# Scores and values on parts of the PE array, pairs of blocks grouped by mode, one array and one transfer for each block

## The chip, the cores and the metric

The kernel runs on one core of a Trainium2 chip. The time is device microseconds of that core, taken without the profiler's help from whole executions. Each kernel also has one profiled execution. Engines: PE is the TensorE matmul, PEld its weight load, DVE VectorE, ACT ScalarE, POOL GpSimd.

## The reference, cut to what matters

Chunked attention, then a mixture of experts with a locality gate. The change touches the attention alone, and what stands between it and the first expert.

```python
# q, k, v: (4 batches, 8 heads, 768, 64); chunk 32, left context 16, right context 8, 8 memory rows
for c in range(seq // 32):
    k_full = concat(mem_k, k[l_start:r_end]);  v_full = concat(mem_v, v[l_start:r_end])
    a = softmax(q[chunk] @ k_full.T / 8);      out[chunk] = a @ v_full
x = out as (4, 768, 512)
for b, s:                                      # routing, one token after the other
    e = argmax(x @ w_gate) if s == 0 or sigmoid(x @ w_local) < 0.5 else the expert of s - 1
    out[b, s] = softmax(x @ w_gate)[e] * (relu(x[b, s] @ w1[e]) @ w2[e])
```

## The kernel before

The kernel works on 32 blocks of three chunks (96 queries). A block's keys are laid out so that 128 rows serve its three chunks. For each block PE computes scores transposed (keys in the partitions), ACT takes the exponential, PE multiplies by the values, which carry a column of ones for the sum, and DVE divides. Blocks go in pairs for the scores, and the routing of a half batch (four blocks) is spread over later blocks. Cut to what the change and the argument touch:

```python
def scores(qt, kt, qb):
    s_ps = sps.tile([P, 2, 512], F32, name="s_ps")
    st = s_ps[:, :, 0:HP * QB].rearrange("p u (a n) -> p u a n", a=HP)
    for a in range(HP):                       # HP = 4 pairs of heads
        for u in range(2):                    # a head's 64 dims: rows 0-63 or 64-127
            h = slice(DH * u, DH * u + DH)
            nc.tensor.matmul(st[:, u, a], lhsT=kt[h, a], rhs=qt[h, a], start=True, stop=True)
    ...                                       # exponentials on ScalarE into pt

def values(pt, vt, n, x):
    for u in range(2):
        o_ps = ops.tile([QB, HP, VW], F32, name="o_ps", tag=f"o_ps{u}")      # one buffer for each half
        for a in range(HP):
            nc.tensor.matmul(o_ps[:, a], lhsT=pt[:, u, a], rhs=vt[:, 2 * a + u], start=True, stop=True)
        rinv = rinvs[:, n, u]
        nc.vector.reciprocal(rinv, o_ps[:, :, DH:VW])
        nc.vector.tensor_tensor(...)          # x = o_ps * rinv

def route_places(r, half):
    nc.vector.tensor_tensor(rank[:, h], rank[:, h], onehot[:, h], op=ALU.mult)
    ...

for n in range(NB):                           # NB = 32 blocks, PAIR = 2
    if n % PAIR == 0:
        for f in first.pop(n, ()): f()        # logits of four finished blocks
        for m in range(n + PAIR, min(n + 2 * PAIR, NB)):
            begun[m] = begin(m)               # scores of the next pair
    ...
    values(begun.pop(n), vts.pop(n), n, xs[b][0:QB, j])
    ...
    if n > 0:
        turn(n - 1)                           # transposes of the block before, and ScalarE's copy
    for f in after.pop(n, ()): f()            # steps of the routing, early plan, first gathers
```

PE's instructions are kept in program order. After the attention come the expert tiles. The rows of the first five are gathered by GpSimd's indirect transfers while the attention still runs.

## Time and profile before

| | before |
|---|---|
| timed runs | 533.83 us, median of 3 (526.76 to 535.96) |
| profiled run | 500.6 us, span 498.5 us, mean granted clock 0.994 |
| PE busy | 485.0 us of the span (97%), 3474 matmul records and as many weight loads |
| attention's end (first expert product, h_ps) | 112.7 us |

### The profile page before, as it was taken

The numbers are of one execution on the slowest core, as the hardware profiler recorded it, in microseconds if no ns is written. First come the engines' busy times: TensorE is split into PE (matmuls) and PEld (weight loads), VectorE is DVE, ScalarE is ACT, GpSimd is POOL, SyncE is SP. The second block draws the span as 40 slices with busy tenths as digits, with TensorE's granted clock in tenths as the row PEclk, the third lists the DMA queues.
The fourth block names the chain that finished last, engine by engine and source line by source line (L and its number), as shares of the span: only waits on it lengthen the run. The fifth ranks groups of instructions, "written<-read, shape, count | busy, mean of one in ns | idle before, by whom it ended". The sixth has DMA issues, their size and how long they took to land. (4 is left out here: it accounts for less than half of the span.)

```text
span 498.5 us, 9231 instructions
## 1 busy us (share of the span) xinstructions
PE 485.0 (97%) x3474; PEld 371.5 (75%) x3474; DVE 109.4 (22%) x437; ACT 111.1 (22%) x234; POOL 99.0 (20%) x151
## 2 busy tenths in 40 slices
PE   8999999999999999999999999999999999999993
PEld 5998888888766777766677776667777666958761
DVE  2456677775435000001000000000000000000000
ACT  4555555542111111111111111110111110201110
POOL 3003222433341122110111111001102110031301
PEclk9999999999999999999999999999999999999997
DMA  8987899999999999998999899995169999921101
GB/s 284 384 268 230 280 280 288 313 352 392 409 328 393 410 408 400 350 313 318 336 333 332 318 322 322 331 339 214 39 214 413 373 400 410 393 70 52 45 29 31
DMA packets 49377, 146.01 MB, mean 293 GB/s; under 512 B 7258, under 2 KB 11358, under 8 KB 49312
## 3 DMA queue, kind: packets, MB, share of 16 engines
q1 hardware_dynamic: 42240, 123.38, 68.6%
q0 software_dynamic: 6784, 21.30, 11.7%
q8 instruction: 34, 0.56, 0.5%
q10 hardware_dynamic: 288, 0.52, 0.3%
q14 instruction: 31, 0.25, 0.1%
HBM read 132.57 MB, written 13.00 MB: 292 GB/s over the span
## 5 line engine op out<-in xcount | busy, mean ns | idle before, releaser
L644 PE MATMUL y_ps<-w_sb,ht 128*128 128x512 f32 x224 | 98.5, 593 | 0.0
L644 PEld LDWEIGHTS h_ps<-held_xt,w_sb 128*128 128x128 f32 x704 | 80.5, 192 | 6.6 <-issue 4.9
L644 PE MATMUL h_ps<-held_xt,w_sb 128*128 128x128 f32 x704 | 81.3, 275 | 0.9 <-ACTq _compat.py:109 0.9
L644 PEld LDWEIGHTS y_ps<-w_sb,ht 128*128 128x128 f32 x224 | 41.5, 190 | 46.9 <-issue 46.6
L796 POOL DMA_INDIRECT out_dram<-y,to x24 | 24.2, 1010 | 240.3 <-ACT y L795 213.2
L780 PEld LDWEIGHTS h_ps<-gxt,w_sb 128*128 128x128 f32 x448 | 51.2, 192 | 2.9 <-issue 2.9
L780 PE MATMUL h_ps<-gxt,w_sb 128*128 128x128 f32 x448 | 51.7, 275 | 0.0
L783 ACT ACTIVATE ht<-h_ps 128x512 f32<-128x512 f32 x42 | 25.1, 597 | 118.9 <-PE h_ps L644 78.1
L791 PE MATMUL y_ps<-w_sb,ht 128*128 128x512 f32 x112 | 49.4, 592 | 0.0
L644 PE MATMUL o_ps<-vt,pt 128*96 128x65 f32 x512 | 49.2, 249 | 0.1
L644 PEld LDWEIGHTS o_ps<-vt,pt 128*96 128x96 f32 x512 | 46.2, 165 | 2.2 <-DVE x L358 0.6
L466 POOL DMA_INDIRECT x_dram<-x,row x32 | 29.6, 926 | 73.9 <-DVE x L464 59.0
L710 DVE COPY held_xt<-g_ps 128x512 f32<-128x512 f32 x12 | 8.3, 689 | 137.5 <-PE g_ps L644 123.0
L791 PEld LDWEIGHTS y_ps<-w_sb,ht 128*128 128x128 f32 x112 | 20.7, 190 | 23.0 <-issue 22.2
L644 PEld LDWEIGHTS s_ps<-qt,kt 64*128 64x128 f32 x512 | 30.2, 189 | 6.8 <-issue 4.6
L644 PE MATMUL s_ps<-qt,kt 64*128 64x96 f32 x512 | 33.0, 279 | 0.4 <-ACT pt L348 0.4
L644 PEld LDWEIGHTS h_ps<-x,w_sb 128*128 128x128 f32 x192 | 31.2, 190 | 1.2 <-issue 1.2
L644 PE MATMUL h_ps<-x,w_sb 128*128 128x192 f32 x192 | 31.9, 327 | 0.0
L348 ACT ACTIVATE pt<-s_ps,mask_mid 128x256 f32<-128x256 f32 x72 | 28.1, 482 | 7.1 <-PE s_ps L644 7.0
L710 DVE COPY gxt<-g_ps 128x512 f32<-128x512 f32 x10 | 6.9, 690 | 95.5 <-PE g_ps L707 52.8
L795 ACT ACTIVATE y<-y_ps,x 128x512 f32<-128x512 f32 x12 | 8.3, 688 | 83.1 <-PE y_ps L644 76.4
L358 DVE TENSOR_TENSOR x<-o_ps,rinvs 96x256 f32<-96x256 f32 x64 | 26.3, 418 | 1.2
(207 smaller groups left out, 375.4 us busy)
## 6 DMA issues: line engine op xcount, KB each, us to landing
w_sb<-in_w_dram SPq DMA_DIRECT2D x192, 512.0 KB, 8.9
vt<-in_v_dram SPq DMA_DIRECT2D x32, 260.0 KB, 4.7
kt<-in_k_dram SPq DMA_DIRECT2D x30, 256.0 KB, 4.9
qt<-in_q_dram SPq DMA_DIRECT2D x32, 192.0 KB, 4.3
kt<-in_k_dram ACTq DMA_DIRECT2D x2, 256.0 KB, 3.3
x_dram<-x,row POOLq DMA_INDIRECT x32, 7.2
out_dram<-y,to POOLq DMA_INDIRECT x24, 7.1
x<-x_dram,rows_late POOLq DMA_INDIRECT x11, 7.2
```

Source lines behind the costliest of these rows:

```text
L348: nc.scalar.activation(pt[:, :, :, c], st[:, :, :, c], ACT.Exp, bias=m[:, g:g + 1], scale=SCALE)
L358: nc.vector.tensor_tensor(x[:, 0:D].rearrange("p (a u d) -> p u a d", u=2, d=DH)[:, u], o_ps[:, :, 0:DH], rinv.to_broadcast([QB, HP, DH]), ...
L466: ins = nc.gpsimd.indirect_dma_start(out=x_dram[:, :], out_offset=bass.IndirectOffsetOnAxis(ap=row[:, n:n + 1], axis=0), in_=x[0:QB, j + n ...
L644: return lambda *a, **k: tc.keep_in_program_order(f(*a, **k))
L710: nc.vector.tensor_copy(xt[:, :, 0:P], g_ps)
L780: nc.tensor.matmul(h_ps[:, m], lhsT=w1_sb[:, kk, P * (g + m):P * (g + m) + P], rhs=xt[:, kk, 0:rows], start=(kk == 0), stop=(kk == DK - 1))
L783: nc.scalar.activation(ht[:, g:g + many], h_ps, ACT.Relu)
L791: nc.tensor.matmul(y_ps, lhsT=ht[:, m, 0:P], rhs=w2_sb[:, m], start=(m == 0), stop=(m == FK - 1))
L795: nc.scalar.activation(y, y_ps, ACT.Copy, scale=xs[:, D:D + 1])
L796: return nc.gpsimd.indirect_dma_start(out=out, out_offset=bass.IndirectOffsetOnAxis(ap=to, axis=0), in_=y, in_offset=None, bounds_check=NT ...
```

## The change

The intent: use the small products better. The scores have only 64 rows to contract, so the array is split into four 64x64 tiles. The values have 96 columns of weights, so they go on three tiles of 32 columns. As a change of tile mode drains PE (from scores to values before, 202 ns pass from last start to first start, against 85 ns within the values), the order is regrouped: both blocks' values, then both transposes, then the routing's transposes. A block's q, k and v become one array and one transfer. Two smaller parts: the ranks are transposed with all 128 rows, and one multiplication of the routing moves from VectorE to GpSimd.

```diff
 def scores(qt, kt, qb):
         for a in range(HP):
-            for u in range(2):
-                h = slice(DH * u, DH * u + DH)
-                nc.tensor.matmul(st[:, u, a], lhsT=kt[h, a], rhs=qt[h, a], start=True, stop=True)
+            for c in (slice(0, DH), slice(DH, P)):
+                for u in range(2):
+                    h = slice(DH * u, DH * u + DH)
+                    nc.tensor.matmul(st[c, u, a], lhsT=kt[h, a, c], rhs=qt[h, a], start=True, stop=True,
+                                     tile_position=(DH * u, c.start))
 def values(pt, vt, n, x):
             for a in range(HP):
-                nc.tensor.matmul(o_ps[:, a], lhsT=pt[:, u, a], rhs=vt[:, 2 * a + u], start=True, stop=True)
+                for g in range(NG):
+                    c = slice(CHUNK * g, CHUNK * g + CHUNK)
+                    nc.tensor.matmul(o_ps[c, a], lhsT=pt[:, u, a, c], rhs=vt[:, 2 * a + u], start=True, stop=True,
+                                     tile_position=(0, CHUNK * g))
 def route_places(r, half):
-        nc.vector.tensor_tensor(rank[:, h], rank[:, h], onehot[:, h], op=ALU.mult)
+        nc.gpsimd.tensor_tensor(rank[:, h], rank[:, h], onehot[:, h], op=ALU.mult)
 def route_rows(r, b, half, x):
-        r_ps = xps.tile([QB, HALF, E], F32, name="r_ps", tag="xps")
+        r_ps = xps.tile([QB, HALF, P], F32, name="r_ps", tag="xps")
-            nc.tensor.transpose(r_ps[:, n], rank[:, ...], identity=ident[:E, :E])
+            nc.tensor.transpose(r_ps[:, n], ranks[:, ...], identity=ident)
 ... (q, k, v as slices of one array qkv; one transfer for each block but the first two)
-    plan_at(after, NB - 3, first_turned)
+    plan_at(after, NB - 2, first_turned)
-    for n in range(NB):
-        ... (logits; scores of the next pair; then for each block: values, transposes, routing)
+    for n in range(0, NB, PAIR):
+        pair = range(n, n + PAIR)
+        for m in range(n + PAIR, min(n + 2 * PAIR, NB)):
+            begun[m] = begin(m)
+        for m in pair:
+            ...
+            values(begun.pop(m), blocks.pop(m)[2], m, xs[b][0:QB, j])
+            ...
+            for f in first.pop(m, ()): f()        # logits, between the two blocks' values
+        for m in range(max(n - 1, 0), n + PAIR - 1):
+            turn(m)
+        for m in pair:
+            for f in after.pop(m, ()): f()
```

More of the change, by code (lines that the diff above doesn't have):

```diff
@@ L46 @@
 LOADS = 6
+KEYS = HP * QB
+VALS = KEYS + HP * P
+BW = VALS + H * VW
 PLAN = 3 * E + 5
@@ L66 @@
     tc: tile.TileContext,
-    q: bass.AP,
-    k: bass.AP,
-    v: bass.AP,
+    qkv: bass.AP,
     w_gate: bass.AP,
@@ L88, with general @@
     nc.gpsimd.iota(back, pattern=[[0, 1], [1, E]], base=-E, channel_multiplier=0, allow_small_or_imprecise_dtypes=True)
-    everything(tc, q, k, v, w_gate, w_local, w1, w2, x_dram, out, ident, back, kept_i)
+    everything(tc, qkv, w_gate, w_local, w1, w2, x_dram, out, ident, back, kept_i)
     kept = nc.values_load(kept_i, min_val=0, max_val=NT * H, skip_runtime_bounds_check_because="a count of sums")
     with tc.If(kept < NT * H):
-        general(tc, q, k, v, w_gate, w_local, w1, w2, out, ident, back)
+        general(tc, qkv, w_gate, w_local, w1, w2, out, ident, back)
 @with_exitstack
-def general(ctx, tc, q, k, v, w_gate, w_local, w1, w2, out, ident, back):
+def general(ctx, tc, qkv, w_gate, w_local, w1, w2, out, ident, back):
     nc = tc.nc
@@ L131, in general @@
             qt, kt, vt = (one.tile([P, a, w], F32, name=t) for t, a, w in (("qt", HP, QB), ("kt", HP, P), ("vt", H, VW)))
-            for t, a in ((qt, q), (kt, k), (vt, v)):
-                nc.sync.dma_start(t, a[n])
+            for t, at in ((qt, 0), (kt, KEYS), (vt, VALS)):
+                _, a, w = t.shape
+                nc.sync.dma_start(t, qkv[n, :, at:at + a * w].rearrange("p (a w) -> p a w", a=a))
             x = one.tile([QB, HP, 2, DH], F32, name="x")
@@ L232, in everything @@
 @with_exitstack
-def everything(ctx, tc, q, k, v, w_gate, w_local, w1, w2, x_dram, out, ident, back, kept_i):
+def everything(ctx, tc, qkv, w_gate, w_local, w1, w2, x_dram, out, ident, back, kept_i):
     nc = tc.nc
@@ L259, in everything, with block, parts, load @@
     nc.gpsimd.dma_start(x_dram[0:1], zeros[0:1].bitcast(I32))
-    def load_qk(n, queue=nc.sync):
-        qt = ld.tile([P, HP, QB], F32, name="qt")
-        nc.sync.dma_start(qt, q[n])
-        kt = ld.tile([P, HP, P], F32, name="kt")
-        queue.dma_start(kt, k[n])
-        return qt, kt
-    def load_v(n):
-        vt = ld.tile([P, H, VW], F32, name="vt")
-        nc.sync.dma_start(vt, v[n])
-        return vt
-    qks = {n: load_qk(n, nc.scalar) for n in range(2)}
-    qks.update({n: load_qk(n) for n in range(2, LOADS - 2)})
-    vts = {n: load_v(n) for n in range(LOADS - 2)}
+    def block():
+        return ld.tile([P, BW], F32, name="block")
+    def parts(t):
+        q, k, v = t[:, 0:KEYS], t[:, KEYS:VALS], t[:, VALS:BW]
+        return (q.rearrange("p (a w) -> p a w", a=HP), k.rearrange("p (a w) -> p a w", a=HP),
+                v.rearrange("p (h w) -> p h w", h=H))
+    def load(n):
+        t = block()
+        nc.sync.dma_start(t, qkv[n])
+        return parts(t)
+    blocks = {}
+    for n in range(PAIR):
+        t = block()
+        nc.sync.dma_start(t[:, 0:KEYS], qkv[n, :, 0:KEYS])
+        nc.scalar.dma_start(t[:, KEYS:VALS], qkv[n, :, KEYS:VALS])
+        blocks[n] = t
+    for n in range(PAIR):
+        nc.sync.dma_start(blocks[n][:, VALS:BW], qkv[n, :, VALS:BW])
+        blocks[n] = parts(blocks[n])
+    blocks.update({n: load(n) for n in range(PAIR, LOADS)})
     wg = once.tile([P, DK, QUARTER], F32, name="wg")
@@ L332, in everything @@
                             base=0, channel_multiplier=-1)
+    ranks = once.tile([P, S], F32, name="ranks")
+    nc.gpsimd.memset(ranks, 0.0)
     def scores(qt, kt, qb):
@@ L432, in route_ranks @@
         of_half = slice(HQ * half, HQ * half + HQ)
-        if half == 0:
-            r["rank"] = sm.tile([E, S], F32, name="rank")
-        onehot, rank = r["onehot"], r["rank"]
+        onehot, rank = r["onehot"], ranks[0:E]
         nc.vector.tensor_tensor_scan(rank[:, of_half], onehot[:, of_half], onehot[:, of_half],
@@ L442, in route_places @@
     def route_places(r, half):
-        onehot, rank = r["onehot"], r["rank"]
+        onehot, rank = r["onehot"], ranks[0:E]
         h = slice(HQ * half, HQ * half + HQ)
-        nc.vector.tensor_tensor(rank[:, h], rank[:, h], onehot[:, h], op=ALU.mult)
+        nc.gpsimd.tensor_tensor(rank[:, h], rank[:, h], onehot[:, h], op=ALU.mult)
         tot = r["tot"] = sm.tile([QB, HALF, 1], F32, name="tot")
@@ L454, in route_rows @@
         j = HALF * half
-        rank, tot, ex = r["rank"], r["tot"], r["ex"][:, j:j + HALF]
-        r_ps = xps.tile([QB, HALF, E], F32, name="r_ps", tag="xps")
+        tot, ex = r["tot"], r["ex"][:, j:j + HALF]
+        r_ps = xps.tile([QB, HALF, P], F32, name="r_ps", tag="xps")
         for n in range(HALF):
-            nc.tensor.transpose(r_ps[:, n], rank[:, QB * (j + n):QB * (j + n) + QB], identity=ident[:E, :E])
+            nc.tensor.transpose(r_ps[:, n], ranks[:, QB * (j + n):QB * (j + n) + QB], identity=ident)
+        r_ps = r_ps[:, :, 0:E]
         row = sm.tile([QB, HALF], I32, name="row", bufs=2)
@@ L649, in begin @@
     def begin(n):
-        ahead = n + LOADS - 2
-        if ahead < NB:
-            qks[ahead] = load_qk(ahead)
-        return scores(*qks.pop(n), n % NQB)
+        return scores(*blocks[n][0:2], n % NQB)
     xs, xts, lts, routes = {}, {}, {}, {}
@@ L734, in everything @@
     begun = {n: begin(n) for n in range(PAIR)}
-    for n in range(NB):
-        b, j = divmod(n, NQB)
-        if n % PAIR == 0:
-            for f in first.pop(n, ()):
-                f()
-            for m in range(n + PAIR, min(n + 2 * PAIR, NB)):
-                begun[m] = begin(m)
-        if j == 0:
-            xs[b] = xp.tile([P, NQB, XW], F32, name="x")
-            nc.gpsimd.tensor_copy(xs[b][0:QB, :, D + 1:XW].bitcast(I32), token[:, n:n + NQB])
-            routes[b] = begin_route()
-        if j % HALF == 0:
-            xts[n // HALF] = sm.tile([P, DK, HALF, QB], F32, name="xt", bufs=2)
-        values(begun.pop(n), vts.pop(n), n, xs[b][0:QB, j])
-        if n + LOADS - 2 < NB:
-            vts[n + LOADS - 2] = load_v(n + LOADS - 2)
-        if n > 0:
-            turn(n - 1)
-        for f in after.pop(n, ()):
-            f()
+    for n in range(0, NB, PAIR):
[3 more added lines that the diff above has]
+        for m in pair:
+            b, j = divmod(m, NQB)
+            if j == 0:
+                xs[b] = xp.tile([P, NQB, XW], F32, name="x")
+                nc.gpsimd.tensor_copy(xs[b][0:QB, :, D + 1:XW].bitcast(I32), token[:, m:m + NQB])
+                routes[b] = begin_route()
+            if j % HALF == 0:
+                xts[m // HALF] = sm.tile([P, DK, HALF, QB], F32, name="xt", bufs=2)
+            values(begun.pop(m), blocks.pop(m)[2], m, xs[b][0:QB, j])
+            if m + LOADS < NB:
+                blocks[m + LOADS] = load(m + LOADS)
+            for f in first.pop(m, ()):
+                f()
+        for m in range(max(n - 1, 0), n + PAIR - 1):
+            turn(m)
+        for m in pair:
+            for f in after.pop(m, ()):
+                f()
     some_pieces(len(early["pieces"]))
@@ L962 @@
     arrays = {
-        "q": dims_first(i["q"]).reshape(B, P, HP, NQB, QB).transpose(0, 3, 1, 2, 4).reshape(NB, P, HP, QB),
-        "k": dims_first(with_mem["k"])[..., bands].transpose(0, 3, 1, 2, 4).reshape(NB, P, HP, P),
-        "v": rows(with_mem["v"])[:, bands].reshape(NB, P, H, VW),
+        "qkv": _np.concatenate([
+            dims_first(i["q"]).reshape(B, P, HP, NQB, QB).transpose(0, 3, 1, 2, 4).reshape(NB, P, HP * QB),
+            dims_first(with_mem["k"])[..., bands].transpose(0, 3, 1, 2, 4).reshape(NB, P, HP * P),
+            rows(with_mem["v"])[:, bands].reshape(NB, P, H * VW)], 2),
         "w_gate": i["moe_w_gate"],
```

## The prediction

> **What bounds the kernel now.** I first read the page's table of busy time in slices: TensorE (PE) is at nine tenths in nearly every slice, and the clock there is full. Then the table of windows: from 0 to about 112 us the attention runs (scores, exponentials, values, routing), and from there to the end the expert tiles, in which PE is busy 10.00 of every 10 us. The change touches only the attention; the expert tiles keep their instructions. So I looked at PE's own timeline over four blocks, the period of the routing:
>
> ```profile
> 53.19 2.03 PE L644 MATMUL s_ps<-qt,kt 64*128 64x96 f32 x32
> 55.15 1.57 PE L644 MATMUL o_ps<-vt,pt 128*96 128x65 f32 x16
> 56.56 0.50 PE L644 MATMUL xt_ps<-ident,x 96*128 96x96 f32 x4
> 56.99 0.35 PE L644 MATMUL r_ps<-ident,rank 8*96 8x8 f32 x4
> 57.63 0.64 PE L644 MATMUL l_ps<-ident,lt_sb 128*96 128x128 f32 x4 [0.29 <-ACT xt L366]
> 58.11 1.49 PE L644 MATMUL o_ps<-vt,pt 128*96 128x65 f32 x16
> 59.44 0.50 PE L644 MATMUL xt_ps<-ident,x 96*128 96x96 f32 x4
> 59.87 2.03 PE L644 MATMUL s_ps<-qt,kt 64*128 64x96 f32 x32
> ...
> 65.77 0.85 PE L644 MATMUL lt_ps<-xt,wg 128*32 128x384 f32 x8
> ```
>
> Columns: start, duration, then the group. The period from scores to scores of four blocks is 53.19 to 66.56, that is 13.37 us, and PE hardly waits in it. Values of one block (o_ps) and of the next are apart by a transpose (xt_ps) and sometimes more. What VectorE (DVE) does with them in the meantime is this:
>
> ```profile
> 56.08 0.18 DVE L357 RECIPROCAL rinvs<-o_ps 96x4 f32<-96x4 f32 x1 [1.19 <-PE o_ps L644]
> 56.29 0.42 DVE L358 TENSOR_TENSOR x<-o_ps,rinvs 96x256 f32<-96x256 f32 x1
> 56.76 0.18 DVE L357 RECIPROCAL rinvs<-o_ps 96x4 f32<-96x4 f32 x1
> 56.97 0.42 DVE L358 TENSOR_TENSOR x<-o_ps,rinvs 96x256 f32<-96x256 f32 x1
> ```
>
> Each half block (u) costs DVE 0.68 us from reciprocal to reciprocal. Each o_ps half has only one PSUM buffer, so the next block's half 0 may start only when L358 has read this block's. Today it starts 1.75 us after it at the closest, and the DVE chain takes about 1.6: it just fits. The third view is the list of groups by shape:
>
> ```profile
> L644 PE MATMUL o_ps<-vt,pt 128*96 128x65 f32 x512 | 49.2, 249 | 0.1
> L644 PE MATMUL s_ps<-qt,kt 64*128 64x96 f32 x512 | 33.0, 279 | 0.4 <-ACT pt L348 0.4
> L644 PE MATMUL yu_ps<-w_sb,x 128*64 128x256 f32 x96 | 11.0, 382 | 0.0
> L644 PE MATMUL lt_ps<-xt,wg 128*32 128x384 f32 x64 | 6.8, 498 | 0.3
> ```
>
> Each product is two instructions (256 score products, 512 records). yu_ps and lt_ps are column tiles already in use.
>
> **What the Trainium skill says.** "TensorE: Matmul & The Clock Gate", section "LDWEIGHTS (loading the stationary operand)", puts a weight load at its columns divided by 1.2 GHz: 80 ns for 96, 107 for 128. The trace agrees: in steady state o_ps instructions start 85 ns apart, and pairs of score instructions 112 ns apart, so both are bound by weight loads, not by streaming 65 or 96 columns. "TensorEngine Tiling (Array Packing)", section "Tiling Modes", says that tiles load and multiply in parallel and that a change of mode drains the engine. The trace agrees: the two column halves of yu_ps start 7 ns apart, one pair every 215.7 ns; lt_ps starts its four quarters 7 ns apart; and where the mode changes, scores to values, 202 ns pass from last start to first start instead of 85. The same page, "PSUM Bottleneck", warns that evacuation may become the limit once the matmuls are faster. This is what I expect here, though no line of before shows it yet.
>
> **The change part by part.** All is for four blocks, two pairs, against 13.37 us.
>
> Scores on 64x64 tiles: four tiles start together. Streaming 96 columns takes 80 ns (yu_ps gives 215.7 for 256, so 0.84 ns a column), loading 64 columns less. One group of four every 84 ns in place of a pair every 112: 16 groups a pair of blocks, 1.28 us to the last start in place of 1.757. Saved: 0.47 a pair, 0.95 in four blocks.
>
> Values on 128x32 tiles: a load of 32 columns is 27 ns, streaming 65 columns 55 to 57. Three tiles every 57 ns in place of one instruction every 85: a half takes 0.46 us in place of 0.68. On PE alone that would be 8 halves x 0.22 = 1.8 us in four blocks. But the changed order puts both blocks' values back to back, and DVE's order of instructions is reciprocal, product, reciprocal, product as before. Counting from the first values instruction T: half 0's last start at T+0.42; DVE takes it up 0.285 later (as the trace has it) at T+0.72, ends at T+1.35; the next block's half 0 starts at T+1.40 instead of T+0.92. Half 1 is done by DVE at T+2.03, the next block's half 1 runs T+2.08 to T+2.5. So the four halves take about 2.5 us, the same as the 2.57 they took before. The gain on values is nearly all lost to DVE.
>
> Grouping by mode: logits (lt_ps) now sit between the two blocks' values, in the same mode, where PE waits for DVE anyway. Before, lt_ps with its waits on both sides takes 0.29 + 0.37 + 0.42 = 1.07 us once in four blocks; it becomes free except for what follows. In that pair the two scans of the ranking (0.94 and 1.00 us on DVE) come before the normalisations in DVE's order, since the transposed choices (c_ps) come at the end of the pair before, so the second block's values start some 0.3 to 0.5 us late: the values phase takes about 3.0.
>
> Transposes: two xt_ps in a row now take both buffers of that PSUM pool, so the third user (c_ps, or r_ps) waits for ScalarE's copy: last start of the first + 0.28 + 0.48 + 0.05 = 0.81, less the 0.43 until it would have started = 0.39 lost a pair, 0.78 in four blocks. r_ps with all 128 rows takes 4 x 125 ns in place of 4 x 55, but saves two drains; l_ps no longer waits 0.29. Together about even. The multiplication moved to GpSimd takes 0.55 us off DVE, in a place where it helps little.
>
> Sum of my table: first kind of pair 1.28 + 0.20 + 2.49 + 0.18 + 0.59 + 0.47 + 0.25 + 0.18 = 5.64; second kind, with logits, 1.28 + 0.20 + 3.0 + 0.18 + 0.59 + 0.47 + 0.38 + 0.12 + 0.37 + 0.18 = 6.77. Together 12.4 in place of 13.37: 0.96 saved, six periods, 5.8 us. The early pairs, with no routing yet, go from 5.48 to about 4.95: 1.2 us more in all.
>
> Lost at two places: the early plan's 25 small DVE operations, which end at 90.5 us before, now stand in front of a normalisation that PE needs sooner, 1.3 us. And the first tile's transposes (first_turned) move to the last pair, so the copy that the first expert product needs stands behind routing on DVE: about 1.4 us.
>
> The transfers: one block of 725 KB in one descriptor row of 5.7 KB in place of three of 1.5 to 2.1 KB. The trace has 65, 84 and 85 ns for the three packets, 234 together; at the 25.7 bytes per ns that the 4 KB weight packets reach, 5664 bytes are 220. That is 6% less DMA time. PE never waits for these loads in the steady state, so it is worth nothing, and at the start blocks 2 and 3 arrive with their values attached, later by about as much as the first scores gain.
>
> Net: 5.8 + 1.2 - 1.3 - 1.4 = 4.3, say 4 to 7 us of about 500 profiled. The timed runs are 7% longer than the profiled one with nothing in the page to say why; if PE's clock is lower there, PE's share of the gain grows a little. I take 6 off 533.8.
>
> **The rivals.** First: PE gets its whole gain, because DVE keeps up (a shorter handover, or the scans out of the way). Then scores 0.95, values 1.8 and logits 1.1 minus the 0.8 of transposes give about 3 us a period, some 23 us: 510. For it speaks that DVE is busy only 9.09 of 13.36 us in the windows view; against it, the single buffer per half and DVE's fixed order. Second: small tiles cannot be issued fast enough. Values would need six instructions in 57 ns; the fastest sustained stretch in before is four in 112. If they came at 14 ns each, values would run as before and scores too: no gain, and with the losses above 535 to 537. For it: instructions fetched grow by 3072. Against: lt_ps and yu_ps start 7 ns apart, though only in short bursts. Third: loads become the bound, as blocks are wanted every 3.1 us instead of 3.3; 725 KB at the 350 to 400 GB/s seen early are 2 us, so no.
>
> **Range and chances.** My sum lies under 2% (10.7 us). For a gain over 2%, rival one must hold at least by half: 0.27. Slower by over 2% would need rival two and lost DMA time: 0.06. The range of 510 to 537 spans rival one in full and rival two, and leaves room for the 9 us by which the three runs before differ.
>
> **What would show it.** In the profile after: score records 21 ns apart on average in place of 56 (84 per four); halves of values about 0.46 us each, but the second block's halves with idle time put down to DVE L380; c_ps or r_ps waiting for ScalarE's xt; periods of 12.4 us; the attention's end at about 107 in place of 112.7; expert tiles at 14.45 us as now. The prediction is wrong if values phases of a pair take 1.9 us with no wait for DVE, or if the score groups stay at 112 ns.

## More of the kernel before

From the page of the profile: PE's busy share and its granted clock, each digit a tenth in a fortieth of the span, and the queue that brings instructions (packets, megabytes, share of the DMA engines).

```profile
PE   8999999999999999999999999999999999999993
PEclk9999999999999999999999999999999999999997
...
q8 instruction: 34, 0.56, 0.5%
```

PE is busy throughout and at full clock. The last line looks like nothing. It is 34 transfers of 16,384 bytes. In the table of the stops below, 1024 more PE records bring about four more of them, so one transfer carries some 256 instructions (an estimate).

## The result, and the profile after

A ratio here is the mean time of one kernel's fast runs over the mean of the other's of the same rounds, so it is not quite the ratio of the medians quoted beside it. Of the four runs of before in this table, two are slow by the rule that a run over 1.5% above the fastest is slow (533.83 and 535.96); the ratio rests on the other two, 522.26 and 526.76.

| | before | after |
|---|---|---|
| timed runs of these rounds | 530.3 us, median of 4 (522.26 to 535.96) | 541.4 us, median of 4 (539.79 to 543.76) |
| ratio | | 1.0326, interval 1.0222 to 1.0429: slower |
| profiled run | 500.6 us, clock 0.994 | 539.79 us, clock 0.971 |
| first expert product | 112.7 us | 151.2 us |

The change makes the kernel slower by 3.3%, and 541.4 lies outside the predicted range. On the chips of the experiments the kernel before takes 499.9 to 500.2 us in every round, and the changed kernel 521.6 and 523.1 (ratios 1.0446 and 1.0455). Why the first chip's timed runs of before were 522 to 536 stays unexplained; its profiled run was 500.6. The quieter chips carry the argument.

The same lines of the page, of the kernel after:

```profile
PE   6688877877699999999999999999999999999993
...
PEclk9999888878899999999999999999999999999998
...
q8 instruction: 45, 0.74, 0.5%
```

All the loss is in the first eleven slices, the attention: PE is idle for one to four tenths of every slice there, and its clock is lowered. The 45 instruction transfers are 11 more than before.

The list of groups by shape, of the kernel after (busy time and mean ns of one, then the idle time before the group and its reasons):

```profile
L666 PE MATMUL o_ps<-block,pt 128*32 128x65 f32 x1536 | 49.1, 246 | 19.6 <-issue 15.4 <-DVE rinvs L379 3.8 <-PE o_ps L666 0.3
L666 PE MATMUL s_ps<-block 64*64 64x96 f32 x1024 | 31.7, 248 | 10.6 <-issue 7.8 <-ACT pt L366 1.8 <-DMA block<-in_qkv_dram 0.8
...
L666 PE MATMUL lt_ps<-xt,wg 128*32 128x384 f32 x64 | 8.0, 535 | 1.1 <-issue 1.1
```

Before, o_ps had 0.1 us of idle time in front of it and s_ps 0.4. Now there are 30 us in all. Of these 3.8 are the wait for DVE that the prediction named. But 23.2 us are "issue": PE waited for nothing that the profile shows.

PE's timeline of the kernel after, first in a bad stretch and then in a good one:

```profile
51.68 0.32 PE L666 MATMUL s_ps<-block 64*64 64x96 f32 x2 [0.35 <-issue]
52.39 0.34 PE L666 MATMUL o_ps<-block,pt 128*32 128x65 f32 x5 [0.39 <-issue]
53.15 0.32 PE L666 MATMUL o_ps<-block,pt 128*32 128x65 f32 x4 [0.42 <-issue]
...
60.99 1.55 PE L666 MATMUL s_ps<-block 64*64 64x96 f32 x64
62.48 1.05 PE L666 MATMUL o_ps<-block,pt 128*32 128x65 f32 x45
...
64.57 1.20 PE L666 MATMUL o_ps<-block,pt 128*32 128x65 f32 x48 [0.34 <-DVE rinvs L379]
```

In the good stretch the tiles run as meant: 64 score matmuls between 60.99 and 62.48, 23 ns each with the change of mode, and the 48 value matmuls of a block in about 1.1 us. The second block's values wait for DVE. In the bad stretch mostly four or five matmuls start every 0.72 us. DVE's own timeline at the end of the bad stretch shows its two operations as long as before, 0.18 and 0.42 us, and DVE waiting for PE:

```profile
56.97 0.17 DVE L379 RECIPROCAL rinvs<-o_ps 96x4 f32<-96x4 f32 x1
57.17 0.42 DVE L380 TENSOR_TENSOR x<-o_ps,rinvs 96x256 f32<-96x256 f32 x1
58.33 0.18 DVE L379 RECIPROCAL rinvs<-o_ps 96x4 f32<-96x4 f32 x1 [0.74 <-PE o_ps L666]
```

Two things had to be told apart: stretches in which PE crawls, and whole stops. The crawl falls into the bursts in which GpSimd issues four indirect transfers (in this stretch at 50.39, 51.72, 52.94 and 54.16 us, each about 0.92 us). It was so only in this chip's run: the changed kernel on two other chips showed only a few gaps of 0.6 to 0.7 us in such bursts. What differs on that chip stays open. The stops appear on all four chips that ran a kernel with tiles of equal width, the first one included, and the experiments below are about them.

### The profile page after: what moved, and what is told of

Its sections match the earlier page's. It is cut to its first block, busy times and chain, and to the rows that moved or that the text cites. A ratio compares the mean times of both kernels' runs of the same rounds, so it can differ in the third digit from the quotient of the medians.

```text
span 538.1 us, 12177 instructions
## 1 busy us (share of the span) xinstructions
PE 491.1 (91%) x5010; PEld 365.9 (68%) x5010; DVE 109.1 (20%) x429; ACT 111.0 (21%) x234; POOL 108.0 (20%) x160
## 3 DMA queue, kind: packets, MB, share of 16 engines
q0 software_dynamic: 6784, 21.30, 11.1%
## 5 line engine op out<-in xcount | busy, mean ns | idle before, releaser
L666 PE MATMUL o_ps<-block,pt 128*32 128x65 f32 x1536 | 49.1, 246 | 19.6 <-issue 15.4
L666 PEld LDWEIGHTS o_ps<-block,pt 128*32 128x32 f32 x1536 | 40.1, 125 | 31.4 <-issue 20.6
L666 PE MATMUL s_ps<-block 64*64 64x96 f32 x1024 | 31.7, 248 | 10.6 <-issue 7.8
L666 PEld LDWEIGHTS s_ps<-block 64*64 64x64 f32 x1024 | 25.2, 133 | 17.0 <-issue 14.5
L729 DVE COPY held_xt<-g_ps 128x512 f32<-128x512 f32 x12 | 8.3, 691 | 137.5 <-PE g_ps L666 123.0
```

The costliest lines, as they stand in the source:

```text
L666: return lambda *a, **k: tc.keep_in_program_order(f(*a, **k))
L729: nc.vector.tensor_copy(xt[:, :, 0:P], g_ps)
```

## The experiments

First state of the theories. **A**: the small tiles need more PE instructions than can be supplied (5665 records before the first expert product in place of 2593), so PE stops for want of instructions. (A record here is a matmul or a weight load.) **B**: the regrouping or the single transfer costs the time, and the tiles are innocent. Later a third was added, **C**: the multiplication on GpSimd is what PE waits for.

Each run has three rounds beside the kernel before on its chip. Shown edits are cut to their core.

### The tiles taken out of the changed kernel (e1, e2, e3), and the kernel before again (e4)

Edit of e1, to the changed kernel:

```diff
-            for c in (slice(0, DH), slice(DH, P)):
-                for u in range(2):
-                    nc.tensor.matmul(st[c, u, a], lhsT=kt[h, a, c], ..., tile_position=(DH * u, c.start))
+            for u in range(2):
+                nc.tensor.matmul(st[:, u, a], lhsT=kt[h, a], ...)
-                for g in range(NG):
-                    nc.tensor.matmul(o_ps[c, a], lhsT=pt[:, u, a, c], ..., tile_position=(0, CHUNK * g))
+                nc.tensor.matmul(o_ps[:, a], lhsT=pt[:, u, a], ...)
```

e2 takes out only the value tiles, e3 only the score tiles, and e4 is the kernel before.

Expected of e1:

> The changed kernel with scores and values back on the old tiles (pairs on row halves, full width), keeping the grouping by pairs, the one array and transfer, the ranks on 128 rows and the multiplication on GpSimd. Theory A (TensorE gets its instructions too slowly: the small tiles start 21 and 19 ns apart only until the supply runs out, and then crawl at 4 matmuls per 0.72 us while GpSimd issues its indirect transfers): no crawl, attention ends near 112 us, time within 1.5% of before, 8 to 9 us of the loss left at most. Theory B (the grouping, with values waiting for VectorE, or the single transfer makes the loss): as slow as the changed kernel, ratio near 1.03.

Expected of e2:

> Only the scores on 64x64 tiles, values full width: 1024 more PE instructions than before (512 matmuls with their loads) instead of 3072. Theory A: part of the loss, crawls only where scores fall into GpSimd's bursts of indirect transfers, ratio 0.99 to 1.015, and faster than the changed kernel by at least 10 us. Theory B: ratio near 1.03.

Expected of e3:

> Only the values on 128x32 tiles, scores on row halves as before: 2048 more PE instructions. Theory A: most of the loss, ratio 1.01 to 1.03, crawls in the values inside GpSimd's bursts. Theory B: ratio near 1.03 here and in the two others alike.

Expected of e4:

> The kernel before itself, for a second trace of it: its profiled run took 500.6 us, its timed runs 522 to 536. Theory A: if the second trace is of a slow execution (over 515 us), it shows the same crawl of TensorE inside GpSimd's bursts of indirect transfers, milder, and a lower granted clock; if it is fast it shows none. Rival: a slow execution shows evenly longer instructions or waits for transfers instead. Ratio to before 1.00 within 2%.

| run | median us | ratio to before | interval |
|---|---|---|---|
| e1, no tiles | 520.5 (median of the four fast runs, 517.3 to 524.1; two slow ones took 552 and 555) | 1.0429 | 1.0384 to 1.0473 |
| e2, only score tiles | 517.09 | 1.0332 | 1.0293 to 1.0372 |
| e3, only value tiles | 517.82 | 1.0343 | 1.0326 to 1.0360 |
| e4, before | 500.23 | 1.0002 | 0.9985 to 1.0019 |

Theory A as stated falls with e1: with no tile at all the changed kernel is about as slow as with them (521.6 us on another chip, e5 below). So something other than the tiles costs some 20 us. e1's profile fell in a slow run, so it isn't used for timings. e4 had only fast runs, so it says nothing of what a slow execution of before looks like. e2's trace has PE waiting twice in front of r_ps for "POOL ranks", 7.8 us in all and 5.8 at the longest. This is the moved multiplication, and it made theory C.

### The changed kernel again (e5), and with the multiplication back on VectorE (e6)

```diff
-        nc.gpsimd.tensor_tensor(rank[:, h], rank[:, h], onehot[:, h], op=ALU.mult)
+        nc.vector.tensor_tensor(rank[:, h], rank[:, h], onehot[:, h], op=ALU.mult)
```

Expected of e5:

> The changed kernel itself, on the chip of this call, where the kernel before should show its 500 us. Theory C (two losses: TensorE waits for the ranks' multiplication, which stands on GpSimd behind indirect transfers, some 8 us with the half clock that follows each; and a crawl of the small tiles inside GpSimd's bursts, which depends on the chip or the execution): 517 to 520 us without a crawl, 535 or more with it. If both tilings gained on their own, it should be 5 us or more below the 517 of the runs with one tiling.

Expected of e6:

> The changed kernel with one line undone: the multiplication of ranks and choices is on VectorE again. Theory C: the two waits of 2.3 and 6.0 us before the ranks' transposes are gone, and the run is 7 to 10 us faster than the changed kernel beside it. Rival: other waits end there instead (VectorE's planning operations, GpSimd's copies), gain under 3 us.

e5 took 521.62 us (1.0446, interval 1.0409 to 1.0483), e6 516.91 (1.0360, interval 1.0323 to 1.0397). The GpSimd move is worth 4.7 us in the changed kernel, by the medians on the same chip; 7 to 10 were expected. Of PE's waits in e5, in the attention (us in all, times, longest):

```profile
PE o_ps L666 <- issue: 10.8, 8, 2.2
PE o_ps L666 <- DVE rinvs L379: 6.9, 12, 1.8
...
PE r_ps L666 <- POOL ranks L466: 4.2, 1, 4.2
```

In e6 the last line is gone, and the "issue" line remains, with 9.4 us. One of these stops in e5's timeline:

```profile
31.79 0.84 PE L666 MATMUL o_ps<-block,pt 128*32 128x65 f32 x33
34.84 0.54 PE L666 MATMUL o_ps<-block,pt 128*32 128x65 f32 x15 [2.20 <-issue]
```

PE halts in the middle of a block's values, after 33 of 48, with all its data there. The trace's transfers show one of the instruction queue from 32.50 to 33.47 us, and PE goes on at 34.83, 1.36 us after its end. This was then looked for in every trace: stops of PE longer than 0.9 us that end 1.15 to 1.6 us after the end of an instruction transfer. A stop is counted from the start of the last matmul to the start of the next, so about 0.2 us of each is still work. They are counted in the table below.

### Tiles alone in the kernel before (e7, e8)

The edit of e7 is the first block of the change's diff, applied to the kernel before; e8 applies the second as well (three tiles of 32 columns).

Expected of e7:

> The kernel before with the scores on 64x64 tiles and nothing else. If the score tiles are sound and the losses come from the grouping and the move to GpSimd: 0.47 us a pair of blocks, 16 pairs, 6 to 8 us faster than before, ratio 0.984 to 0.988. If the supply of instructions is short: ratio 1.00 or above, with gaps in TensorE inside the score groups.

Expected of e8:

> The kernel before with both tilings, its own order kept, so values and transposes change mode each time. From the durations: values 0.4 us a block less, two more drains of about 0.1, so 5 to 8 us on top of the score tiles, ratio 0.970 to 0.978. If VectorE's chain or the supply of instructions binds: not faster than with the score tiles alone.

e7 took 494.91 us (0.9898, interval 0.9878 to 0.9918), e8 514.20 (1.0283, interval 1.0265 to 1.0301). Score tiles alone make the kernel 1% faster than before, which is clear of noise but less than the 6 to 8 us that were expected. Adding the value tiles makes it 19.3 us slower, with no regrouping, no single transfer and no GpSimd move in it. So the tiles aren't innocent either. VectorE's chain is ruled out as the cause in e8: its trace has no wait for DVE's rinvs at all. e7's one stop, and then the line of the waits of e8:

```profile
20.97 0.64 PE L646 MATMUL o_ps<-vt,pt 128*96 128x65 f32 x5
23.31 1.15 PE L646 MATMUL o_ps<-vt,pt 128*96 128x65 f32 x11 [1.70 <-issue]
```

```profile
PE o_ps L649 <- issue: 17.8, 11, 4.0
```

### Values on two column tiles (e9, e10)

The next question was whether fewer instructions would be free of stops. The first try cuts the 96 columns into 64 and 32.

```diff
-                nc.tensor.matmul(o_ps[:, a], lhsT=pt[:, u, a], rhs=vt[:, 2 * a + u], start=True, stop=True)
+                for c in (slice(0, DH), slice(DH, QB)):
+                    nc.tensor.matmul(o_ps[c, a], lhsT=pt[:, u, a, c], rhs=vt[:, 2 * a + u], start=True, stop=True,
+                                     tile_position=(0, c.start))
```

e10 has the score tiles too.

Expected of e9:

> The kernel before with the values on two column tiles (columns 0 to 63 and 64 to 95) in place of one instruction of 96: 1024 more PE instructions instead of 2048 for three tiles, and the same streaming time (65 columns, 57 ns). Theory D (TensorE runs out of instructions: it stops until 1.2 to 1.5 us after a 16 KB instruction transfer ends, whenever 256 of them are used up faster than the next transfer comes): about as many instructions as with the score tiles alone, so few stops, 0 to 3, and 2 to 6 us faster than before. Rival (the change of mode at every transpose, or VectorE's chain, makes the values' tiles slow): as slow as both tilings with three tiles, 510 or more.

Expected of e10:

> Score tiles and values on two column tiles, in the order of before: 2048 more PE instructions. Theory D: between 495 and 514, with 4 to 9 stops after instruction transfers in place of 13; near 503. Rival: 514 as with three tiles, since modes and VectorE's chain are the same.

e9 took 587.27 us (1.1712; one of its four runs slow), e10 577.99 (1.158). A miss for the question, but a clear fact: tiles of two widths do not overlap. By shape, in e9:

```profile
L646 PE MATMUL o_ps<-vt,pt 128*64 128x65 f32 x512 | 84.3, 247 | 0.0
L646 PE MATMUL o_ps<-vt,pt 128*32 128x65 f32 x512 | 77.2, 233 | 0.0
```

A product is two matmuls (512 records for 256 products). In the trace they start at 13.112 and 13.220 us on the tile of 64 columns, at 13.372 and 13.452 on that of 32, at 13.602 again on that of 64. So each tile takes 230 to 260 ns, one after the other, and a block's 32 matmuls take about 3.9 us (16 pairs of 245 ns) where 16 full ones took 1.4. Going from one width to the other takes 150 ns from start to start, against 80 and 108 ns within a width. It looks like the drain at a change of mode that the prediction quotes: here every product is such a change. On the supply of instructions the runs say only one thing: e10 has as many PE records as e14 below and not one stop, but needs much longer for them.

### The rest without tiles and without the GpSimd move (e11), and the move alone (e12)

e11 is e1 with the multiplication on VectorE, so what stays of the change is the grouping, the single transfer and the transposes of 128 rows. e12 is the kernel before with only the multiplication on GpSimd.

Expected of e11:

> Only the grouping by pairs, the single transfer and the ranks on 128 rows: no small tiles, the multiplication on VectorE. It holds the cost of the grouping alone. From the trace with tiled scores (4 blocks in 13.39 us with the scores' 0.95 saved), 13.9 to 14.3 us for four blocks in place of 13.37, so 5 to 7 us, and the first expert tile's copy 1.1 us, the plan 3 us: 508 to 512. If it is at 500, the grouping is free and the loss lies with the move to GpSimd and the instructions alone.

Expected of e12:

> The kernel before with the ranks' multiplication on GpSimd and nothing else. It stands behind the five early gathers (6 us of GpSimd) once and behind GpSimd's wait for the token copy once: 3 to 8 us slower than before, with TensorE's ranks' transposes (or what follows in its order) waiting for GpSimd. Rival: the order of before has more slack, and it costs under 1 us.

e11 took 510.62 us (1.0218, interval 1.0200 to 1.0237), e12 511.65 (1.0211, interval 1.0172 to 1.0249). Both parts cost about 2% each on their own; as the intervals lie across the 2% mark, the verdict on each is unclear, though both are slower beyond noise. e12 lost more than the 3 to 8 us expected. The timeline of GpSimd in e12, and below it PE's:

```profile
99.01 0.94 POOL L603 DMA_INDIRECT xs<-x_dram,rows_early  x1 [0.30 <-issue]
99.97 0.98 POOL L446 TENSOR_TENSOR rank<-rank,onehot 8x384 f32<-8x384 f32 x1
```

```profile
96.38 0.50 PE L644 MATMUL xt_ps<-ident,x 96*128 96x96 f32 x4
101.00 0.48 PE L644 MATMUL r_ps<-ident,rank 8*96 8x8 f32 x4 [4.13 <-POOL rank L446]
101.42 1.09 PE L644 MATMUL l_ps<-ident,lt_sb 128*96 128x128 f32 x4
```

In this trace GpSimd runs what it is given in order. Five gathers of the first expert tiles, issued from 93.96 us on, each 0.94 to 0.99 us with 0.30 between them, stand in front of the multiplication, which itself takes 0.98 us against 0.55 on VectorE. PE needs its result and waits 4.13 us. Afterwards l_ps takes 1.09 us where it took 0.64: the clock has dropped. The Trainium skill, "TensorE: Matmul & The Clock Gate", section "What's actually happening", says that PE's clock is halved after an idle window of some 3.4 us. This trace agrees: after 4.13 us of waiting, the granted clock is 0.50 from 100.72 to 117.78 us. So most of what e12 loses by the first expert product (11.1 us against e4) is not the wait itself but the 17.1 us at half clock after it, up to half of whose length is lost (an estimate: 8.5 us). Other traces go further than the page: in e5 the clock is 0.50 for 3.41 us from 35.23 us on, though PE's longest pause before it was 2.20 us and PE had been busy for 1.2 of the 3.41 us before.

Five consecutive steps of e11's timeline, the second kind of pair, with logits:

```profile
57.15 1.57 PE L661 MATMUL o_ps<-block,pt 128*96 128x65 f32 x16
58.65 0.85 PE L661 MATMUL lt_ps<-xt,wg 128*32 128x384 f32 x8
59.44 1.57 PE L661 MATMUL o_ps<-block,pt 128*96 128x65 f32 x16
60.85 0.83 PE L661 MATMUL xt_ps<-ident,x 96*128 96x96 f32 x8
61.91 0.64 PE L661 MATMUL r_ps<-ident,ranks 128*96 128x128 f32 x4 [0.24 <-ACT xt L383]
```

Four blocks take 14.29 us here (scores at 55.19 and 69.48) in place of 13.37. Its lateness against before (e4's trace, start of each pair's scores) grows by 0.7 us up to the fifth pair, 4.0 more to the 13th, 3.3 around the early plan (13th to 16th pair), and 3.2 from there to the first expert product: 11.2 in all.

### Values on two equal tiles (e13), with score tiles (e14), and the changed kernel a third time (e15)

To keep one mode, the second tile has 64 columns as well. The last 32 of them are other data or zeros, and their output isn't read. The results stay right. To have the columns behind a head there, both runs also keep the exponentials in four fixed buffers.

```diff
-            o_ps = ops.tile([QB, HP, VW], F32, name="o_ps", tag=f"o_ps{u}")
+            o_all = ops.tile([P, HP, VW], F32, name="o_ps", tag=f"o_ps{u}")
+            o_ps = o_all[0:QB]
             for a in range(HP):
-                nc.tensor.matmul(o_ps[:, a], lhsT=pt[:, u, a], rhs=vt[:, 2 * a + u], start=True, stop=True)
+                at = (u * HP + a) * QB
+                for c in (0, DH):
+                    nc.tensor.matmul(o_all[c:c + DH, a], lhsT=pt[:, at + c:at + c + DH], rhs=vt[:, 2 * a + u],
+                                     start=True, stop=True, tile_position=(0, c))
```

Expected of e13:

> The kernel before with the values on two equal column tiles of 64 (the second holds 32 wanted queries and 32 columns of the next head, which nothing reads): 1024 more PE instructions, as many as with the score tiles alone. Supply theory: 0 to 2 stops after instruction transfers, 494 to 499 us. Rival (mode changes or VectorE's chain): 505 or more, without stops at the instruction transfers.

Expected of e14:

> Score tiles and values on two equal tiles of 64: 2048 more PE instructions against 3072 of the run with three value tiles (514 us), with the same durations, modes and order. Supply theory: fewer stops than that run's 13, 495 to 506 us. Rival: 514 again.

Expected of e15:

> The changed kernel a third time. If this chip gives it the crawl (4 matmuls per 0.72 us inside GpSimd's bursts), about 540 us or 1.08 times before; if not, about 521, ratio 1.044. No theory says beforehand which chip does it.

e13 took 494.66 us (0.9903, interval 0.9884 to 0.9922), e14 503.36 (1.0066, interval 1.0017 to 1.0114), e15 523.08 (1.0455, interval 1.0438 to 1.0473). This is the sharpest test of the supply: score tiles save 5.0 us alone, value halves 5.4 alone, both on the same path, so together they should give some 490. They give 503.4, within the 495 to 506 expected of the supply theory. From the waits of e14, in the attention:

```profile
PE o_ps L657 <- issue: 5.1, 4, 2.1
PE s_ps L657 <- issue: 3.5, 5, 1.3
```

No wait for DVE's rinvs is among e14's waits, nor among e13's, so VectorE's chain does not explain the difference.

### Score tiles with the single transfer (e16)

The edit of e7 on the kernel before, with the change's one array and one transfer.

Expected of e16:

> The kernel before with the score tiles and the single array and transfer per block, nothing else of the change. Against 494.9 us with the score tiles alone: if the transfer is hidden as predicted, the same within 2 us; at the start, values attached to blocks 2 and 3 may cost up to 1 us.

e16 took 498.24 us (0.9978, interval 0.9917 to 1.0039), 3.3 more than e7 by the medians of two chips; its runs spread from 496.8 to 502.7, so the size isn't sharp. In its trace the fourth block's scores wait for the one transfer at the start (0.85 us where e7's waited 0.20 for ScalarE), and its lead over before shrinks later. The single transfer doesn't help and seems to cost a few microseconds, against the "same within 2 us" expected.

### The stops in all traces

Worked out from each trace: the time of the first expert product, the transfers of the instruction queue up to the end of the values, the records (matmuls and weight loads) before the first expert product, the stops as defined above, and how long the granted clock was 0.50 before the first expert product.

| kernel | first expert product, us | transfers | records | stops | us in them | us at half clock |
|---|---|---|---|---|---|---|
| before (e4) | 111.8 | 10 | 2593 | 0 | 0 | 0 |
| e12 multiplication on GpSimd | 122.9 | 10 | 2593 | 0 | 0 | 17.1 |
| e11 grouped, no tiles | 123.0 | 10 | 2593 | 0 | 0 | 0 |
| e7 score tiles | 107.1 | 14 | 3617 | 1 | 1.9 | 0 |
| e13 value halves | 106.4 | 14 | 3617 | 0 | 0 | 0 |
| e16 score tiles, one transfer | 111.5 | 14 | 3617 | 1 | 1.0 | 0 |
| e2 after, score tiles only | 128.2 | 14 | 3617 | 1 | 1.2 | 10.2 |
| e3 after, value tiles only | 129.6 | 17 | 4641 | 4 | 5.5 | 10.2 |
| e14 score tiles and value halves | 115.3 | 18 | 4641 | 5 | 8.0 | 6.8 |
| e10 both tiled, 64 and 32 columns | 188.3 | 18 | 4641 | 0 | 0 | 0 |
| e6 after, multiplication on VectorE | 129.3 | 21 | 5665 | 9 | 15.2 | 13.7 |
| e5 after | 130.4 | 21 | 5665 | 9 | 15.4 | 13.7 |
| e15 after | 137.7 | 21 | 5665 | 7 | 14.0 | 23.9 |
| after, first chip, with the crawl | 151.2 | 21 | 5665 | 4 | 5.9 | 27.3 |
| e8 both tiled, before's order | 127.6 | 22 | 5665 | 13 | 23.6 | 10.2 |

The window of 1.15 to 1.6 us was chosen after the first stops were seen, but it is narrow: it covers 3 to 8% of the attention's time. On the quiet chips 49 of the 50 pauses over 0.9 us (from start to start) that the profile puts down to "issue" end inside it, and one of the pauses that have a named cause (e5 at 99.55 us, put down to DVE, 2.0 us; it is one of e5's nine).

The last column is a second cost. Each stretch at half clock lasts 3.41 us or a multiple of it (e12's 17.1 is five times that); before each of them PE had been busy for at most 2.1 of the 3.41 us. What PE does then takes up to twice as long, so up to half of that time is lost beside the stops (an estimate: 6.8 us in e5).

On the quiet chips the stops grow with the records, whatever the order of the blocks, unless the records come slowly (e10). The transfers follow the records (2593 records, 10 transfers of 256). The trace also suggests why it happens mostly when both products are tiled. Value tiles start 19 ns apart, each with a weight load, so 256 records are used up in 128 x 19 = 2.4 us, score tiles in 128 x 21 = 2.7. In the kernels with both, no two instruction transfers start closer together than 3.35 us (e15 3.36, e5 3.35, e8 3.43); a transfer itself takes 0.88 us or more. Over a while the mean demand is below this rate, since transposes and waits lie between; it seems to be the runs of scores and values in a row that outrun it. That it is the fetch that limits is an inference from these coincidences: nothing in the profile names the reason of a stop, and what in the fetch takes the 1.2 to 1.6 us after a transfer isn't shown. Nor was it tested whether other transfers delay the fetch: the instruction transfers of e8 took from 0.88 to 2.4 us.

## Why the prediction was wrong, by its own steps

The ladder on the quiet chips, by medians: 500.0 before; 510.6 with grouping, single transfer and 128-row ranks (e11, +10.6); 516.9 with the tiles added (e6, +6.3); 521.6 with the multiplication on GpSimd (e5, +4.7). The parts interact, so in another order they would have other sizes. The tiles alone cost 14.3 in the order of before (e8), the GpSimd move 11.6 (e12).

**Tile rates: right.** "One group of four every 84 ns" and "Three tiles every 57 ns": the records are 21 and 19 ns apart. Score tiles alone save 5.0 us; the prediction's 0.47 a pair would make 7.5 in 16 pairs, less the one stop of 1.9. The 27 ns for a load of 32 columns, an estimate from the skill's formula, was not measured apart.

**"Second: small tiles cannot be issued fast enough": this rival was put aside wrongly, and this is the step that failed most.** Instead of the two tilings saving time, they cost 6.3 us in the changed order and 14.3 in that of before. Its "for", 3072 more instructions, is what the stops follow in the table; its "against", starts 7 ns apart "though only in short bursts", was no evidence for long bursts, as the text itself said. The form was other than thought: the tiles don't come at 14 ns each but at full rate, and then not at all for 1 to 4 us (for want of instructions, as inferred above). The stops take 15.4 us (e5) of the changed kernel's attention. In e6 they take 15.2 while the tiles' net cost is 6.3, so by subtraction the tiles save about 8.9 and pay 15.2; in e8 it gives 23.6 - 14.3 = 9.3 saved. These are estimates, and low ones: they leave out what the half clock costs.

**"The gain on values is nearly all lost to DVE": right in the changed order, and not a law.** In the pairs of e5 that neither a stop nor routing disturbs, 0.60 to 0.69 us pass from the last start of the first block's values to the first start of the second's; the prediction put the delay at 0.48 (T+0.92 to T+1.40). In e5 PE waits 12 times for DVE, 6.9 us. In the order of before, where transposes lie between, the value halves save 5.4 us (e13), with no wait for DVE's rinvs.

**"The multiplication moved to GpSimd takes 0.55 us off DVE, in a place where it helps little": wrong in sign.** It looked only at the engine that it left. On the engine where it arrived it takes 0.98 us and queues behind five gathers, and PE waits 4.1 to 4.2 us for it at the early gathers, with a halved clock around and after it (6.8 us of it in e5, 17.1 in e12). It costs 4.7 us in the changed kernel, 11.6 alone.

**Grouping, "together about even", and the wait for ScalarE, "0.39 lost a pair": the mechanism was right, the sum too small.** The wait measured 0.24 us of PE idle time at c_ps or r_ps (e11). But with full-width values (e11) four blocks take 14.29 us, not less than 13.37: the logits cost PE 0.79 us between the values, which the prediction had free because PE would wait for DVE there; with full-width values PE doesn't wait there. The plan, predicted at 1.3, is worth 3.3 between the 13th and 16th pair, and the end, predicted at 1.4, 3.2. A second stretch, at 117.66 us, has PE waiting 1.02 us for a normalisation behind DVE's routing, which the prediction did not see. How much of the 4.0 us of the steady part would go away with value tiles was not measured apart.

**The transfer, "worth nothing": off, though not sharply.** e16 is 3.3 us slower than e7. The prediction's remark that blocks 2 and 3 arrive later at the start is seen there: 0.85 us at the fourth block's scores.

**"Expert tiles as now": right.** The span after the first expert product is 385.7 us in e4 (497.5 - 111.8) and 386.6 in e5 (517.0 - 130.4).

**Attention's end "at about 107": 130.4 in e5, 151.2 on the first chip.** The first chip's trace has fewer stops (5.9 us) but the crawl under GpSimd's bursts and 27.3 us at half clock. How the difference divides between these was not worked out; the crawl, which no step foresaw and no experiment explains, appeared on one chip only.

Two versions beat both kernels: score tiles alone (e7, 494.9 us) and value halves alone (e13, 494.7 us), each 1% below before and 5% below the changed kernel.

## What to carry to other kernels

Small tiles multiply the instructions, so count the instructions of the longest uninterrupted stretch beside the engine's rate: here one of two tilings was a gain of 1% and both together a loss. A pause costs more than its length where it halves the clock. Before an operation moves to an idle-looking engine, look at what stands in front of it there in order, above all transfers that the engine issues itself. And undo each part of a bundled change separately: here the removal of all tiles showed hardly any difference (e1), for without their stops the move to GpSimd cost more (about 10 us by e1 and e11, 4.7 by e5 and e6).

## What the Trainium skill lacked or had wrong

- "Runtime: NRT & Kernel Launch", section "Instruction fetch mechanics", calls the cost of crossing a block of 16 KiB "mostly hidden". Its block size agrees (every transfer of the queue has 16,384 bytes). The cost does not: with both products on small tiles PE stopped 9 times for 15.4 us (e5) and 13 times for 23.6 us (e8), each stop ending 1.2 to 1.6 us after such a transfer.
- "TensorEngine Tiling (Array Packing)" lists what tiling gains and a fixed overhead of each matmul, but not that records rise with the tiles (2593 to 5665 here), nor a rate at which they can be kept up: 256 in 2.4 us were too fast, and transfers never came closer than 3.35 us.
- The same page says that a change of mode drains, without a figure: 202 ns from last start to first start against 85 within a mode. Nor does it say that column tiles of unequal width, 64 and 32, don't overlap: about 245 ns for each tile's two matmuls, and a kernel 17% slower (e9).
- "TensorE: Matmul & The Clock Gate" does not say how busy PE may be in a window whose end still halves the clock: in e5 it was busy for 1.2 of 3.41 us, with no pause over 2.20 us, and in the traces of the table for up to 2.1.
- No page looked up has the cost of a tensor operation behind indirect transfers on GpSimd: five of them at 0.94 to 0.99 us with 0.30 between, and PE waited 4.13 us (e12).
